# Another instruction order for a layernorm, multi-query attention and SiLU feed-forward kernel: the table that sets the order is replaced

## The chip, the core and the metric

The kernel runs on one core of one Trainium2 chip. The metric is the device time of one execution in microseconds (us), from three executions. TensorE is called PE in the profile, VectorE DVE, ScalarE ACT, GpSimd POOL and SyncE SP; PEld is the loading of weights into PE.

## What is computed

```python
def _A_ref(x, wq, wk, wv, wo):              # S 2048, D 640, H 32 heads of Dh 20, one key and value head
    q = (x @ wq).reshape(B, S, H, Dh).transpose(0, 2, 1, 3)
    k = x @ wk
    v = x @ wv
    scores = jnp.einsum("bhqd,bkd->bhqk", q, k) * (Dh ** -0.5)
    p = _softmax(scores, axis=-1)
    o = jnp.einsum("bhqk,bkd->bhqd", p, v)
    return o.transpose(0, 2, 1, 3).reshape(B, S, H * Dh) @ wo

def _B_ref(x, w1, w2):                      # F 1728
    return jnp.einsum("bsf,fd->bsd", _silu(jnp.einsum("bsd,df->bsf", x, w1)), w2)

xn = _layernorm(x, axis=-1)
return x + _A_ref(xn, A_wq, A_wk, A_wv, A_wo) + _B_ref(xn, B_w1, B_w2)
```

## The kernel before, in words

**The work and its pieces.** The 32 heads are taken in 8 groups of 4, and the 2048 queries in 4 chunks of 512, which makes 32 attention groups. Each attention group runs over 16 key tiles of 128. One *item* is one head, one key tile and 512 queries: a score matrix of 128 keys by 512 queries, which fills one of the 8 banks of PSUM (tile `psall`). There are 2048 items.

- **Scores (S), L1211.** An item's scores are one matmul that uses 32 of PE's 128 rows (a head has 20 channels). Matmuls for four different heads stand in four different row groups and run side by side. In the order they read `MATMUL psall<-sbt 128x512`.
- **Exponential, on ACT or on DVE.** Most items go to ACT: one ACTIVATE (L1301) takes one, two or three neighbouring banks (512, 1024 or 1536 columns). The others go to DVE and POOL: DVE makes an exponential by integer arithmetic from one bank (L1533, called p1), and for each four such items two shifted copies are made, either both on POOL (L1572) or one of them on DVE (L1577). The three copies weighted together correct the coarse exponential.
- **Weighted values (PV), L1336.** Four matmuls of 512 columns, one for each head of a group, side by side in four column groups of PE. One such set belongs to each key tile done by ACT, and three to each key tile done by DVE, one for each copy.
- **Projections and feed-forward, L536** (and L823): all in sets of four matmuls in the four column groups. q, h (first feed-forward layer), out (second layer and output projection together), and for the last query chunk y, w and fin. ACT makes a tanh (L862) and DVE a product (L865) for each bank of h.

PE thus runs in two ways: **row mode** for scores (four row groups) and **column mode** for nearly all else (four column groups). A set of four in either mode streams 512 columns. In the order printed below, a run of scores stands as one row, for instance `L1211 ... x4`: four scores, for ACT and DVE together.

**What sets the order.** The program is straight-line, 22826 instructions in the profile. `build` holds a planner: it keeps a clock for each engine, reckons with a duration for each instruction (`t_act`, `t_dve`, `t_mc`, the table `WAY` for the way from one engine to another, `SWITCH` for a change of PE's mode), and puts instructions in a fixed sequence for each engine; `emit` then writes these sequences with the semaphore waits between them. After 36000 ns on the planner's clock (`HAND`) the planner no longer chooses: PE's sequence is read from the string `ORDER`, and `OTHERS` says in which order DVE, ACT and POOL take the kinds of their instructions. A token of `ORDER` has three characters. `S24` is a run of scores for ACT into two banks from bank 4 on, `S3x` and `S1x` into three and one; `D32` or `E12` is one score for DVE (E: with one of the shifted copies on DVE); `a`, `d` are a set of PV for a key tile of ACT or DVE; `n` begins a job of projection or feed-forward, `m` is its next set. The number of S, D and E tokens also sets how many items go to ACT and how many to DVE.

Where the clocks enter while `ORDER` is followed: an instruction's earliest start, and so which engine's next token is placed first. What runs on the chip is only the resulting sequence of each engine; the chip knows none of the planner's times.

**The end.** The last attention group ends with its last PV. ACT then copies the sums (L1434), PE adds up over the heads (`sum31`, L1132), DVE takes reciprocals (L1135), PE spreads them (`spread31`, L1150), DVE multiplies (L1159), and PE ends the five output banks (`fin0` to `fin4`, in part before and in part behind the spread, L536). DVE (L1100) and for bank 0 ACT and POOL (L1096, L1097) make the result, and four DMAs store it (L1117).

The lines on which most hangs:

```python
def t_act(n):                                     # L250
    return 64.0 + 0.8333 * n
def t_mc(n):                                      # L258: a column set
    return n / 2.4 + (9.0 if n >= 512 else 4.0)
    def turn(self, mode):                         # L347: a change of PE's mode
        return SWITCH[mode] if mode != self.pe_mode else 0.0
        if e == "pe" and not replay["on"] and not replay["at"] and ORDER and sc.t["pe"] >= HAND and cur_job[0] is None and not pro:
            replay["on"] = True                   # L2217: from here ORDER is followed
```

Of the kernel before, what the change touches and what calls it, by code (L numbers as in the profile page):

```python
# [22 lines left out]
QW = 512  # L23
# [35 lines left out]
DVE_END = 85.0  # L59
# [22 lines left out]
SWITCH = {"s": 97.0, "p": 98.0, "f": 98.0}  # L82
SPRIO = 0.5
# [28 lines left out]
def rule(n):  # L112
# [4 lines left out]
    "D32D13S14a97nq6m00m00D25S20m00m00S22D34aa7S20Dd5nh6m00D04D22S13m00m00m00S20S14Dd5G33nh2m00m00m00m00S25D00D31nh4m00m00m00m00ab7S25D20S13nh2m00m00m00m00"  # L117
    "S25Dc1D14nh0m00m00m00m00ac7S21D23s25ad7ae7af7d04d14S31D30d34d24D85D16S17a04d44d64S10S21D33d54a14d94S25E20D97d74dc4S22D01d84df4S25D20D97a24da4nh1m00S22"
    "E30m00D05D26S17m00m00S22E30a34a44db4S25Dc7di4dd4S22D20dl4nh1m00S35de4S10D32Dc3m00m00dg4dj4m00S25E12S17nq0m00m00m00m00dh4S22D35D81a54a64S26D10a74S22D75"
    "nh1m00m00m00m00S25D20S17nh2m00m00dk4m00m00S25D11S13dm4nh7m00m00m00dn4m00S30D85G26nh3m00m00m00m00S24D27s20D12a06a16a26a36d06S24D33Da7d16d36S20D02d26d66"  # L120
    "S23D35a46d46S20E12D87a56d96d56S33D32d86S20D17a66dc6nh2m00S23Dc5D77m00m00m00da6S20E25d76nh3m00m00S24Dc7m00S20D12m00a76nq7m00S24D72m00m00db6m00S20D23a86"
    "S24D82a96df6S20D13E27de6dd6nh2S24D33m00D10E21S17m00m00m00S33S10nh7dh6m00m00m00dg6m00S11S24Db3a02a12d02d32d12S20D13D26d62d22S24D07a22a32S13S20Da6a42d52"
    "nh7m00m00S23D05D16m00m00a52d92d82S20D33De4a62S25d42d72da2S20D33De7dc2S25D04a72nh3m00S20D77m00S24E16m00m00S17D10De1a82db2S24E06a92dd2S20D17de2nh3m00S24"
    "D06m00m00aa2m00S26S10Da1F34nh5m00m00m00m00S22D06a07d07d37S20D34d27d17S22D15a17d67S20Da4D36d57d97S22D05a27d77S20Da4nh6m00m00S22D15m00a37S20D34d87D05E12"
    "S13m00nh4m00m00S20Dd5a47m00m00S22D06d47a57dc7S20D26Dd5da7df7S22E34db7S20D26a67dd7S24D02nh3m00m00S20Dd6m00a77S24E32de7dg7m00S20D26a87nq2m00m00S25D04m00"
    "m00S20D93a97dh7d04S25D32d14S20D23a04d34d24S25D02E37d64S20D93a14nh2m00S25D07m00D23S10D81m00m00a24S35D33nh0m00m00m00m00a34d54S31s25D17d94d74dc4d84d44D20"
    "S21E33a44da4Dc7S25D10a54db4S21D23nh7m00E35Dc0S16m00m00m00S21D13a64df4S25D30dd4nh3m00S21E27m00Dc0S15D26a74m00m00S21D17a84de4S25D30nh7m00S21D83m00m00S25"
    "D20a94dh4S31dg4m00a05d05d35d65D14s16S31nq0m00m00m00m00S26D34a15d25S21D90D23a25d15d45D04S26d55d95S20D92D63a35d75S26D34d85nq2m00S20Dd3m00S26D04m00m00S20"
    "D63a45a55S26E32D04dc5da5db5S20Dd2D63a65df5S26E34nq2m00S20Dd3m00m00S26D04m00a75S20D63a85dd5S26E32de5dg5S20D94a95dh5S22D06E37nq4m00S20D25m00m00S22D06m00"
    "a07d07S20D95d37d67S22D34D06d27S20D25a17a27S32G36d57a37d97S20S25d87dc7a47d17S22Da4F00D11d47d77a57S24Dc6G30S22da7D11S24Dc6a67df7D20s31db7S24D56a77E30s31"  # L130
    "Dc6de7D20S24G36a87S30a97dh7S34dd7dg7nq3m00m00m00m00S20D22a07d07S25D14D83a17d37S20D32d17d47S25D14D83a27d27S20D22d67E34s25D13a37d57S20D22d97a47S23D85G36"
    "S20D22d77da7a57S23D15dc7S20E36d87S22Dc4D15a67df7S20D26db7S22Dc4D55a77S20S16F34a87S22D25de7S20E34F86D15dh7S32a97dd7S20dg7d06d36S32D35G27a06a16S20D95d66"
    "S22D04D37d16no5m00m00m00S20E24m00m00S22D87m00m00m00D14S20m00m00m00d26m00S22S14D87m00m00m00m00m00a26a36S30D33m00a46a56d96d56S24D27d46S20D32Dc3d76da6d86"
    "S24D12E27a66dc6S20D33db6S24D12no7m00m00m00m00S20Dc3m00m00m00m00S24E22a76S20D33m00m00m00m00m00m00S32D25m00m00m00m00a86a96S20E15df6S22Da4D37dd6dg6S20D05"
    "no4m00de6S22Da7m00m00dh6S20D15m00m00m00m00S22D37Da6m00m00m00a05m00S20D07m00a15S22D76d05d15S20D17d35d25S22Da6m00m00a25S20D07m00m00m00m00S22D76a35d65S20"
    "E14D07d55d45S22De6a45a55S20E14D07a65d95S22D36d75d85S20E14Dc7dc5da5S22D26df5db5D14S20D87a75a85a95no2S23E36de5S20D17m00m00m00m00m00S23S26m00m00m00m00m00"
    "m00dh5S20D23D34m00m00m00m00dd5S26D83m00m00m00S20D24dg5a03S26D12a13a23a33S20E34Da5d03d33S26D02a43d13S20D34d63S35E12a53d23nq4m00S20Dc2m00m00m00S25D17d93"
# [60 lines left out]
    "port": (  # L198
        "ppppdpppppddpppddppppppdppdpppdpppddpppppdppppdppppddppppppddppppppdddpppppppdpppppdddppppddddppppdppppddppppdddpppdpdppppdppppppdddppppddpppppddpppdp"
        "ppppppdddpdppppppdddpppppdpdppppppppddpppdppppdpppppdpppppppdddppppddppppppppdddppdppppppddpppddpppppdddpppppddppppdppppdpppppdppppddppdddpppdpppppppp"  # L200
        "pdddppppppdddppppdppdpppppppppdddppppppddppdpdppppdppppdpdppppppppdppppdpppppdppddppppdpdp"),
}
ENDLEAD = 0.04
ENDFROM = 0.85
# [45 lines left out]
def t_act(n):  # L250
    return 64.0 + 0.8333 * n
# [2155 lines left out]
```

## Time and profile before

| what | value |
|---|---|
| time, median of 3 executions | 671.14 us (671.09 to 672.52) |
| the profiled execution's own time | 671.75 us |
| its span, first to last instruction | 669.9 us |
| granted PE clock | 1.0 |
| matmuls, score matmuls among them | 9919, 2048 |
| score items on ACT (527 of two banks, 62 of three, 88 of one) | 1328 |
| score items on DVE | 720 |

The span is the time between the first and the last instruction of the execution that the hardware profiler recorded; 1.85 us lie around it. A busy share is the union of an engine's recorded instructions. Instructions of one engine overlap in the record, since the next begins while the last one still writes: how long an engine is held by one is read from start to start, not from the mean duration. The ends of PE's matmuls are modelled.

### The profile page before, as it was taken

To read this page: it belongs to the slowest core of one execution; us is meant where nothing else is said; L and a number is where in the kernel's file an instruction comes from. 1 tells how busy PE (TensorE), PEld (TensorE's weight loads), DVE (VectorE), ACT (ScalarE), POOL (GpSimd) and SP (SyncE) were. 2 spreads that over 40 slices of the span, in tenths; PEclk is the share of its full clock that TensorE was granted. 3 is DMA by queue.
4 is the path that set the end of the run, shared out by engine and by line. 5 is a ranking of instruction groups with operands and counts; after the bars stand their busy time and mean duration, and the time that the engine had idled before them with its cause. 6 is when DMAs were issued, how large, how long until landed. Compare 5 with 4: busy or idle time off the path is not lost.

```text
span 669.9 us, 22826 instructions
## 1 busy us (share of the span) xinstructions
PE 660.0 (99%) x9919; PEld 240.1 (36%) x9919; DVE 632.8 (94%) x1103; ACT 652.7 (97%) x750; POOL 535.5 (80%) x322
## 2 busy tenths in 40 slices
PE   8999999999999999999999999999999999999997
PEld 5433332332223333333332333333333333344434
DVE  7899999999999999999999999999999999988885
ACT  6999999999999999999999999999999999999995
POOL 6647879888777888977889788878878888778863
PEclk9999999999999999999999999999999999999999
DMA  8652202222131223223222231122422202242021
GB/s 229 169 198 19 30 18 23 23 27 31 26 35 24 34 19 40 30 31 37 63 23 26 26 40 26 24 32 33 77 21 24 21 21 33 22 79 24 9 23 41
DMA packets 34242, 28.99 MB, mean 43 GB/s; under 512 B 15486, under 2 KB 29662, under 8 KB 34142
## 3 DMA queue, kind: packets, MB, share of 16 engines
q1 hardware_dynamic: 33854, 27.20, 26.6%
q8 instruction: 78, 1.28, 0.8%
q10 hardware_dynamic: 288, 0.33, 0.1%
q14 instruction: 22, 0.18, 0.1%
HBM read 11.09 MB, written 2.62 MB: 20 GB/s over the span
## 4 chain that ended last, share of the span: by engine, by line
PE 79%; ACT 10%; DVE 8%; POOL 1%; issue 0%; DMA 0%; DVEq 0%; POOLq 0%; ACTq 0%
PE psall L1336 28%; PE psall L1211 25%; PE psall L536 24%; ACT sbt L1301 9%; DVE sbt L1533 5%; DVE sbt L1577 1%; POOL sbt L1572 1%; PE psall L710 1%; PE psall L684 1%; DVE sbt L782 0%; DVE sbt L1385 0%; DMA sbt<-in_A_x_dram 0%; PE psall L1150 0%; PE psall L1132 0%; DVE sbt L1100 0%
## 5 line engine op out<-in xcount | busy, mean ns | idle before, releaser
L1301 ACT ACTIVATE sbt<-psall 128x1024 bf16<-128x1024 f32 (+2 forms) x677 | 622.7, 1042 | 3.7 <-PE psall L1211 2.7
L1572 POOL TENSOR_SCALAR sbt<-sbt 128x2048 int16<-128x2048 int16 x250 | 474.3, 1897 | 94.3 <-DVE sbt L1577 25.1
L1533 DVE TENSOR_SCALAR sbt<-psall 128x512 int16<-128x512 f32 x720 | 458.1, 681 | 21.0 <-PE psall L1211 16.4
L1336 PE MATMUL psall<-sbt 128*32 128x512 bf16 x3488 | 274.4, 384 | 0.8 <-POOL sbt L1572 0.2
L1211 PE MATMUL psall<-sbt 32*128 32x512 bf16 x2048 | 251.1, 384 | 2.8 <-ACT sbt L1301 1.1
L536 PE MATMUL psall<-sbt 128*32 128x512 bf16 (+4 forms) x3904 | 216.9, 331 | 0.1
L1211 PEld LDWEIGHTS psall<-sbt 32*128 32x128 bf16 x2048 | 69.1, 91 | 222.0 <-ACT sbt L1301 137.3
L536 PEld LDWEIGHTS psall<-sbt 128*32 128x32 bf16 x3904 | 84.5, 95 | 82.6 <-issue 40.2
L1336 PEld LDWEIGHTS psall<-sbt 128*32 128x32 bf16 x3488 | 71.0, 94 | 108.3 <-issue 73.9
L1577 DVE TENSOR_SCALAR sbt<-sbt 128x2048 int16<-128x2048 int16 x110 | 74.6, 710 | 0.2
L949 POOL TENSOR_TENSOR sbt<-sbt 128x512 bf16<-128x512 f32 x30 | 38.3, 1275 | 19.6 <-DVE sbt L1577 17.3
L865 DVE SCALAR_TENSOR_TENSOR sbt<-sbt,psall 128x512 bf16<-128x512 bf16 x52 | 35.2, 677 | 0.2
L862 ACT ACTIVATE sbt<-psall 128x512 bf16<-128x512 f32 x52 | 32.9, 633 | 0.0
L1385 DVE COPY sbt<-psall 128x512 f32<-128x512 f32 x31 | 21.2, 682 | 0.8 <-PE psall L1336 0.6
L782 DVE TENSOR_SCALAR sbt<-psall 128x512 bf16<-128x512 f32 x20 | 13.6, 680 | 0.5 <-PE psall L536 0.3
L661 POOL TENSOR_TENSOR sbt<-sbt 128x2 f32<-128x2 f32 x8 | 5.7, 708 | 8.6 <-DVE sbt L659 8.2
L992 DVE SCALAR_TENSOR_TENSOR sbt<-psall,sbt 128x320 bf16<-128x320 f32 x24 | 11.6, 485 | 0.6 <-PE psall L536 0.6
L674 POOL TENSOR_SCALAR sbt<-sbt 128x640 bf16<-128x640 bf16 x12 | 10.4, 874 | 1.5 <-DVE sbt L666 1.5
L652 DVE BATCH_NORM_STATS2 sbt<-sbt 128x6 f32<-128x320 bf16 x14 | 6.6, 473 | 2.0 <-DMA sbt<-in_A_x_dram 1.9
L684 PE MATMUL psall<-sbt 128*128 128x128 bf16 x80 | 6.9, 220 | 1.1 <-DVE sbt L677 1.1
L1835 PE MATMUL psall<-sbt 128*32 128x256 bf16 x144 | 6.8, 353 | 1.2 <-DVE sbt L576 1.2
L696 DVE COPY sbt<-psall 128x640 bf16<-128x640 bf16 x14 | 6.4, 482 | 1.0 <-PE psall L684 1.0
(59 smaller groups left out, 97.8 us busy)
## 6 DMA issues: line engine op xcount, KB each, us to landing
sbt<-sbt SPq DMA_DIRECT2D x120, 64.0 KB, 3.8
sbt<-in_A_x_dram SPq DMA_DIRECT2D x28, 160.0 KB, 3.9
sbt<-sbt SPq DMA_DIRECT2D x213, 20.0 KB
out_dram<-sbt SPq DMA_DIRECT2D x14, 160.0 KB, 1.9
sbt<-in_B_w_dram SPq DMA_DIRECT2D x1, 2160.0 KB, 12.2
sbt<-in_B_w_dram SPq DMA_DIRECT2D x1, 2080.0 KB, 8.1
sbt<-sbt SPq DMA_DIRECT2D x75, 8.0 KB
sbt<-in_A_wq_dram SPq DMA_DIRECT2D x1, 800.0 KB, 6.3
```

Source lines behind the costliest of these rows:

```text
L536: ins = pe.matmul(ps[j * SLOT:(j + 1) * SLOT, b * BANK + off:b * BANK + off + n], w[:, j * SLOT:(j + 1) * SLOT], x, start=start, stop=stop ...
L782: op = Op("dve", lambda v: v.tensor_scalar_mul(q_st[:, st, :], bk(job.bank), QSCALE), t_dve(512), DVE_END, pre=[job.ready], writes=[res("q ...
L862: t = Op("act", lambda a: a.activation(t_buf[0:rows, ts, :], bk(job.bank, 0, QW, rows=rows), AF.Tanh, scale=0.5), t_act(512), ACT_END, pre ...
L865: u = Op("dve", lambda v: v.scalar_tensor_tensor(out=hT[par][0:rows, fk, :], in0=t_buf[0:rows, ts, :], scalar=1.0, in1=bk(job.bank, 0, QW, ...
L949: nm = pool(lambda e: e.tensor_tensor(oU[:, us, :], U_sb[:, us, :], Rrep, ALU.mult), 1356.0, POOL_END, pre=[uc] + lc + pack_op.get(divmod( ...
L1211: return pe.matmul(bk(b), kT_rep[i * SLOT:(i + 1) * SLOT, kt * P:(kt + 1) * P], qT[i * SLOT:(i + 1) * SLOT, g % NQ, :], start=True, stop=T ...
L1301: return a.activation(Ebuf[:, es * QW:es * QW + w], ps[:, buf[0] * BANK:buf[0] * BANK + w], AF.Exp, scale=ESCALE)
L1336: ins = pe.matmul(ps[i * SLOT:(i + 1) * SLOT, ub * BANK:ub * BANK + QW], lhsT, rhs, start=(first and k < HG), stop=(last and k >= len(lst) ...
L1385: return v.tensor_copy(U_sb[:, us, :], bk(ub))
L1533: p1 = Op("dve", lambda v: v.tensor_scalar(z16[:, i * QW:(i + 1) * QW], bk(job.bank), ZBIAS, 0.0, ALU.add, ALU.max), t_dve(QW) + 2.0, DVE_ ...
L1572: op = pool(lambda v, t=t, j=j, zin=zin: v.tensor_scalar(t.bitcast(I16), zin, float(SHIFT[j]), 1.0, ALU.add, ALU.mult), POOL_SHIFT, POOL_E ...
L1577: op = dve(lambda v, t=t, j=j, zin=zin: v.tensor_scalar_add(t.bitcast(I16), zin, float(SHIFT[j])), t_dve(N, 4), prio=SPRIO - 0.01 * j, **args)
```

## The change

The strings `ORDER` and `OTHERS` are replaced, and with them some of the durations by which the planner reckons while it follows them. The diff, with the strings cut to the start of one (they differ from the first token on):

```diff
-WAY = {("act", "dve"): 32.0, ("dve", "pool"): 84.0, ("pe", "act"): 41.0, ("pe", "dve"): 72.0}
+WAY = {("act", "dve"): 32.0, ("dve", "pool"): 84.0, ("pe", "act"): 42.0, ("pe", "dve"): 72.0}
+HOT = {"on": False}
+FIRST = 10.0
 ORDER = (
-    "D32D13S14a97nq6m00m00D25S20m00m00S22D34aa7S20Dd5nh6m00D04D22S13m00m00m00S20S14Dd5G33nh2m00m00m00m00S25D00D31nh4m00m00m00m00ab7S25D20S13nh2m00m00m00m00"
+    "S12D33D14a97nq6m00m00S15S20D23m00m00nh2m00S23Dc5m00S16D30D11m00m00S23D35nh0m00m00m00m00D21S25Fc4S13nh2m00m00m00m00S25D10aa7ab7ac7S23D20E31ad7S25Dc2ae7"
...
 def t_act(n):
-    return 64.0 + 0.8333 * n
+    return (54.0 if HOT["on"] else 64.0) + 0.8333 * n
...
 def t_mc(n):
-    return n / 2.4 + (9.0 if n >= 512 else 4.0)
+    return n / 2.4 + (3.0 if HOT["on"] else 9.0 if n >= 512 else 4.0)
...
     def turn(self, mode):
-        return SWITCH[mode] if mode != self.pe_mode else 0.0
+        return (106.0 if HOT["on"] and mode == "s" else SWITCH[mode]) if mode != self.pe_mode else 0.0
...
                 start += self.turn(op.mode)
+                if HOT["on"] and op.mode != "s":
+                    op.occ += FIRST
...
-                t_dve(HALF) + 40.0, DVE_END, pre=[job.ready, xres_op[(qc, i)]] + [norm_op[n] for n in range(NT)], reads=[res("xres", i)], writes=[res("os", sl) if hf == 0 else res("os2", sl)],
+                t_dve(HALF), DVE_END, pre=[job.ready, xres_op[(qc, i)]] + [norm_op[n] for n in range(NT)], reads=[res("xres", i)], writes=[res("os", sl) if hf == 0 else res("os2", sl)],
...
-        op = Op("pe", f, 224.0, pre=[x[1] for x in d.values()] + v_op[kt // 4],
+        op = Op("pe", f, t_mc(QW) if HOT["on"] else 224.0, pre=[x[1] for x in d.values()] + v_op[kt // 4],
...
+    HOT["on"] = False
...
+            HOT["on"] = True
             replay["on"] = True
```

No instruction is of a new kind, and none changes its operands' sizes. Up to the first token of `ORDER` the sequences of all engines are the same. From there on they differ nearly everywhere. Counted over the whole program:

| instructions | before | now |
|---|---|---|
| ACT exponentials of two banks | 527 | 532 |
| ... of three banks | 62 | 65 |
| ... of one bank | 88 | 77 |
| DVE exponentials (p1) | 720 | 712 |
| shifted copies on DVE | 110 | 108 |
| shifted copies on POOL | 250 | 248 |
| PV matmuls | 3488 | 3472 |
| score matmuls | 2048 | 2048 |
| runs of scores between other matmuls (rows of L1211 in PE's order, L1215 now) | 591 | 573 |

All other groups have the same counts. Line numbers of the changed kernel are higher by 4 in this part of the source.

The first place is PE just behind the point from which the table rules, while projections of q (L536, now L540) stand between the scores (L1211, now L1215) and PV (L1336, now L1340). Before:

```order
L1336 MATMUL psall<-sbt 32x512 x4
L536 MATMUL psall<-sbt 32x512 x12
L1211 MATMUL psall<-sbt 128x512 x3
L536 MATMUL psall<-sbt 32x512 x8
L1211 MATMUL psall<-sbt 128x512 x3
L1336 MATMUL psall<-sbt 32x512 x4
L1211 MATMUL psall<-sbt 128x512 x3
L536 MATMUL psall<-sbt 32x512 x8
L1211 MATMUL psall<-sbt 128x512 x3
L536 MATMUL psall<-sbt 32x512 x12
```

And now:

```order
L1340 MATMUL psall<-sbt 32x512 x4
L540 MATMUL psall<-sbt 32x512 x12
L1215 MATMUL psall<-sbt 128x512 x4
L540 MATMUL psall<-sbt 32x512 x16
L1215 MATMUL psall<-sbt 128x512 x3
L540 MATMUL psall<-sbt 32x512 x4
L1215 MATMUL psall<-sbt 128x512 x3
L540 MATMUL psall<-sbt 32x512 x8
L1215 MATMUL psall<-sbt 128x512 x3
L540 MATMUL psall<-sbt 32x512 x20
```

The first run of scores shown takes four instead of three, sixteen column matmuls follow it instead of eight, and one PV set has left this place.

The second place is ACT, some 25 rows into its own order: the tanh of the first feed-forward layer (L862, now L866) between exponentials (L1301, now L1305) of one, two and three banks. Before:

```order
L1301 ACTIVATE sbt<-psall 128x1024
L862 ACTIVATE sbt<-psall 128x512
L1301 ACTIVATE sbt<-psall 128x1024
L1301 ACTIVATE sbt<-psall 128x512
L862 ACTIVATE sbt<-psall 128x512
L1301 ACTIVATE sbt<-psall 128x1024
L862 ACTIVATE sbt<-psall 128x512
L1301 ACTIVATE sbt<-psall 128x1024 x2
L1301 ACTIVATE sbt<-psall 128x1536
L1301 ACTIVATE sbt<-psall 128x512 x2
```

And now:

```order
L1305 ACTIVATE sbt<-psall 128x512
L866 ACTIVATE sbt<-psall 128x512
L1305 ACTIVATE sbt<-psall 128x1024 x5
L866 ACTIVATE sbt<-psall 128x512
L1305 ACTIVATE sbt<-psall 128x1024 x7
L866 ACTIVATE sbt<-psall 128x512
L1305 ACTIVATE sbt<-psall 128x1024 x4
L866 ACTIVATE sbt<-psall 128x512
L1305 ACTIVATE sbt<-psall 128x1024 x8
L1305 ACTIVATE sbt<-psall 128x512
```

The tanh instructions stand further apart, and fewer exponentials of one bank lie between them.

The third place is the end of PE's order, from the last run of scores on: `w4` and `fin0` (L536 with 32x512 between PV), the last PV, `fin1` (pieces of 128 and 384), `sum31` (L1132, now L1136) and `spread31` (L1150, now L1154). Before:

```order
L1211 MATMUL psall<-sbt 128x512 x3
L1336 MATMUL psall<-sbt 32x512 x4
L536 MATMUL psall<-sbt 32x512 x4
L1336 MATMUL psall<-sbt 32x512 x16
L536 MATMUL psall<-sbt 32x512 x8
L1336 MATMUL psall<-sbt 32x512 x4
L536 MATMUL psall<-sbt 32x128 x4
L536 MATMUL psall<-sbt 32x384 x4
L536 MATMUL psall<-sbt 32x128 x4
L536 MATMUL psall<-sbt 32x384 x4
L1132 MATMUL psall<-sbt 128x4 x4
L1150 MATMUL psall<-sbt 32x128 x16
```

And now:

```order
L1215 MATMUL psall<-sbt 128x512 x3
L1340 MATMUL psall<-sbt 32x512 x12
L540 MATMUL psall<-sbt 32x512 x4
L1340 MATMUL psall<-sbt 32x512 x4
L540 MATMUL psall<-sbt 32x512 x8
L1340 MATMUL psall<-sbt 32x512 x8
L540 MATMUL psall<-sbt 32x512 x8
L1136 MATMUL psall<-sbt 128x4 x4
L1154 MATMUL psall<-sbt 32x128 x16
L540 MATMUL psall<-sbt 32x128 x4
L540 MATMUL psall<-sbt 32x384 x4
L540 MATMUL psall<-sbt 32x128 x4
```

`fin0` has moved behind the last PV, and `fin1` from there to behind the spread; two more sets of `w4` stand before the last PV.

More of the change, by code (lines that the diff above doesn't have):

```diff
@@ new lines @@
+        "pppppspouppppppppppsspphhpphppsppphpphpphppuhppppppppppppphpphsphphpppppsshpuhqpppppppppppppppppsssopppppupqppppppppppppssspppsppoppppppsuppoppppppppp"
+        "pppsppppqppppppupppssopppppspppppppppssspoppppupsppopppppppppppppsqpppppsssppopupppppppppppqppppppppspppuppopppppppppppsshppppphpphsshpuppphpphpphppss"
+        "ppppppppppshpphpphphppupppshppppppppphpphhpssppppopppppppsspupoppppppspppppppppsspppopppupppsppopppppppposppppppppopuppsppoppppppopppsppppsupypppppppp"
+        "ypppppspppppyppppupppppypppwppwppwpswppssuppspyppppspppsgsw"),
@@ L202 @@
+        "ddppdpppdppppppdddpppppdddppppdppppddpppdppppppppppdpppddpppppppdddpppppppdddpdpppdpppppdpppppddppdpppdddpppdpppppdppdddppppppppdppppppddpppddpppppddp"
+        "ppdpppppdpppppddppppddpppdpppddppppdpppppdpppppdpppppdppdpppppppdppppppppppdppdddpdpdd"),
 }
```

152 lines of the change are left out of this document (73 added, 79 removed).

## The prediction

> **What bounds the kernel now.** The page's head and its shares come first.
>
> ```profile
> span 669.9 us, 22826 instructions
> PE 660.0 (99%) x9919; PEld 240.1 (36%) x9919; DVE 632.8 (94%) x1103; ACT 652.7 (97%) x750; POOL 535.5 (80%) x322
> PE 79%; ACT 10%; DVE 8%; POOL 1%; issue 0%; DMA 0%; DVEq 0%; POOLq 0%; ACTq 0%
> ```
>
> Three engines look full, so the busy shares settle nothing: they are unions of instructions that overlap in the record. The third row, the shares of the chain that ended last, says that 79% of the way back from the end runs over PE, 10% over ACT and 8% over DVE. To see how full an engine is, one must take its pace from start to start. For ACT these rows of the timeline stand side by side:
>
> ```profile
> 483.24 1.10 ACT L1301 ACTIVATE sbt<-psall 128x1024 bf16<-128x1024 f32 x1
> 484.14 0.69 ACT L862 ACTIVATE sbt<-psall 128x512 bf16<-128x512 f32 x1
> ...
> 502.40 1.45 ACT L1301 ACTIVATE sbt<-psall 128x1536 bf16<-128x1536 f32 x1
> 503.74 0.59 ACT L862 ACTIVATE sbt<-psall 128x512 bf16<-128x512 f32 x1
> 504.22 1.03 ACT L1301 ACTIVATE sbt<-psall 128x1024 bf16<-128x1024 f32 x1
> ```
>
> Two banks hold ACT for 484.14 - 483.24 = 0.90 us although the record shows 1.10; three banks for 503.74 - 502.40 = 1.34; one bank for 504.22 - 503.74 = 0.48. That is some 0.43 a bank and 0.05 an instruction. The groups of ACT in the stretch from 36 to 640 us, which the table rules and which has no tail in it:
>
> ```profile
> L1301 ACT ACTIVATE sbt<-psall 128x1024 bf16<-128x1024 f32 x498 | 473.7, 1061 | 1.4 <-PE psall L1211 0.9
> L1301 ACT ACTIVATE sbt<-psall 128x1536 bf16<-128x1536 f32 x54 | 79.7, 1479 | 0.3 <-PE psall L1211 0.2
> L1301 ACT ACTIVATE sbt<-psall 128x512 bf16<-128x512 f32 x84 | 51.5, 627 | 0.2
> L862 ACT ACTIVATE sbt<-psall 128x512 bf16<-128x512 f32 x52 | 32.9, 633 | 0.0
> ```
>
> 498 x 0.90 + 54 x 1.34 + (84 + 52) x 0.48 = 585.8 us of 604. ACT is thus 97% full, and some **18 us of waiting** hide in the overlaps, where the last column shows only 1.9. Here is what one such wait looks like (timeline, all engines):
>
> ```profile
> 565.24 3.95 ACT L1301 ACTIVATE sbt<-psall 128x1024 bf16<-128x1024 f32 x4
> ...
> 566.07 0.82 PE L1336 MATMUL psall<-sbt 128*32 128x512 bf16 x12
> ...
> 566.82 0.10 PEld L1211 LDWEIGHTS psall<-sbt 32*128 32x128 bf16 x4 [0.42 <-ACT sbt L1301]
> 566.82 0.40 PE L1211 MATMUL psall<-sbt 32*128 32x512 bf16 x4
> ```
>
> Four exponentials without a wait would take 3 x 0.90 + 1.10 = 3.80; they took 3.95. The first ended near 565.24 + 1.10 = 566.34 and freed its banks, yet the scores for these banks start at 566.82. In between PE was not idle: it streamed three PV sets from 566.07 on. The scores came late because the order had put them behind that work. The weight load's own wait (0.42 for ACT) had long ended by then. So PE's sequence, more than the length of ACT's work, holds ACT here.
>
> **The change, part by part.** Everything before the first token is the same, so only sums behind it count. PE's pace stands in these rows:
>
> ```profile
> 299.76 0.39 PE L536 MATMUL psall<-sbt 128*32 128x512 bf16 x4
> ...
> 300.09 0.39 PE L1211 MATMUL psall<-sbt 32*128 32x512 bf16 x3
> ...
> 300.42 0.61 PE L1336 MATMUL psall<-sbt 128*32 128x512 bf16 x8
> ...
> 300.96 0.44 PE L1211 MATMUL psall<-sbt 32*128 32x512 bf16 x4
> ```
>
> The second of two column sets ends 0.22 behind the first (0.61 against 0.39). A set before scores holds PE for 300.09 - 299.76 = 0.33, and scores before a set for 300.42 - 300.09 = 0.33. Each turn from one mode to the other thus costs 0.33 - 0.22 = 0.11, and a run of scores two turns, 0.22. PE has 18 runs fewer (591 to 573): 18 x 0.22 = 4.0. It has 16 PV matmuls fewer, four sets: 4 x 0.22 = 0.9. **PE: -4.9 us.** [...]
>
> ACT takes 8 items more, in 3 instructions fewer: 5 x 0.90 + 3 x 1.34 - 11 x 0.48 = +3.2. **ACT: +3.2 us.** DVE's pace:
>
> ```profile
> 174.09 3.67 DVE L1533 TENSOR_SCALAR sbt<-psall 128x512 int16<-128x512 f32 x6
> 177.68 1.28 DVE L1577 TENSOR_SCALAR sbt<-sbt 128x2048 int16<-128x2048 int16 x2
> 178.88 0.24 DVE L940 RECIPROCAL sbt<-sbt 128x16 f32<-128x16 f32 x1
> ```
>
> (177.68 - 174.09) / 6 = 0.60 for a p1 and (178.88 - 177.68) / 2 = 0.60 for a copy. 8 p1 and 2 copies fewer: **DVE -6.0 us.** POOL makes two copies fewer and is 80% busy; I take nothing for it, because what hides a later POOL is the spread between a copy and its PV, and that cover is not thinner with fewer copies.
>
> The **tail** is a term of its own:
>
> ```profile
> 661.08 0.40 PE L1336 MATMUL psall<-sbt 128*32 128x512 bf16 x4
> ...
> 661.31 0.61 PE L536 MATMUL psall<-sbt 96*32 96x128 bf16 x16
> 661.53 0.66 ACT L1434 ACTIVATE sbt<-psall 128x256 f32<-128x256 f32 x2 [0.50 <-PE psall L1336]
> 661.97 0.97 PEld L1132 LDWEIGHTS psall<-sbt 128*128 128x128 f32 x8 [0.33 <-ACT sbt L1434]
> ...
> 663.85 2.59 PE L536 MATMUL psall<-sbt 96*32 96x256 bf16 x72
> 664.74 2.48 DVE L1100 SCALAR_TENSOR_TENSOR sbt<-psall,sbt 128x512 bf16<-128x512 f32 x4 [0.21 <-PE psall L536]
> ```
>
> Between the last PV (661.08) and `sum31` (661.97) PE waits for ACT's copy, and `fin1` (the x16) fills the gap at no cost. In the new order `fin0`, two sets, fills it, and `fin1` stands in the last stretch, behind the spread, where PE runs without a break (the x72) and DVE follows it. `fin1` takes about 0.61 less the 0.2 by which a record outlasts its set: **+0.4 us**. That `fin0` leaves its old place gains nothing, since two `w4` sets take it, in the shadow of the last exponential.
>
> What these loads make of the time depends on who is last, and no row says that for an order that has not run. Two readings bound it. **By the chain's shares**, each engine's change counts with its share of the chain: 0.79 x -4.9 + 0.10 x +3.2 + 0.08 x -6.0 = -4.0. **By ACT alone**, as the fullest engine, it is +3.2. The share of the chain is nearer to what the rows show (PE streaming while ACT waits, a place of the kind at which PE has become lighter), but a lighter PE hands part of the chain to ACT, which has grown. So I give the chain's reading three parts in four: 0.75 x -4.0 + 0.25 x 3.2 = -2.2. With the tail -1.8, from the profiled execution's own 671.75 to 669.95; the median of the runs shown lies 0.61 lower, so the forecast is 671.14 - 1.8 = **669.3 us**. This asks that ACT's hidden waiting falls from 18 to some 18 - 3.2 - 2.2 = 12.6 us.
>
> Two things in the order speak for that much: runs of one bank leave ACT only 0.48 of work while the next scores are made, and there are 11 fewer of them; and the tanh instructions, whose scores need five column sets on PE first, stand further apart on ACT.
>
> **The rivals.**
>
> *ACT takes back all that PE gives (no change).* If the waits shrink by just as much as ACT's work grows, 3.2 and the tail's 0.4, the time stays: 671.1, give or take 1.3. For it: PE and ACT share 8 banks, and a lighter PE waits more often for ACT, as it does 375 times already:
>
> ```profile
> PEld psall L1211 <- ACT sbt L1301: 137.3, 375, 0.6
> PEld psall L1211 <- DVE sbt L1533: 37.7, 104, 0.9
> ```
>
> Most of these waits lie under running matmuls, like the one above.
>
> *ACT is the bound (slower).* The place is the stretch to 640 us, where 97% of ACT's time is work. If the order places scores no better than the old one did, the 18 us of waiting stay, and 3.2 + 0.4 = 3.6 are added: 671.14 + 3.6 = **674.7 us**. It decides when the waits shrink by less than 2.3 us, for then the time is up by over 1.3. Against it speaks that DVE, which holds the other part of the banks, and PE become lighter at once. [...]
>
> *The order fits much better.* If half of the 18 us goes: -9.0 + 3.6 = -5.4, 665.7 us. For it speaks only that waits like the one shown are a matter of sequence, not of work.
>
> *The table does not do what it says.* A sequence fixed beforehand meets durations that differ from those reckoned with. If a score is placed to be just in time and a copy or DMA lands later, PE stalls in order and both engines lose; then the time is that of the slower rival or above it.
>
> **How the numbers follow.** A gain of over 0.2% (1.3 us, about what a measurement of this kernel can tell from no change) comes from the forecast and from the better fit: 0.40 and 0.08. No change: 0.26. Slower: 0.26, the table's failure with it. The likeliest case alone spans 667.1 (the chain's reading without ACT's part, 671.14 - 4.0) to 669.8. The range must reach into both rivals: down to 666.2, a little short of the better fit, and up to 673.8, where the waits shrink by 0.9 only.
>
> **What would show it right or wrong.** The PE groups of the changed kernel must show the same 0.22 and 0.33; if a turn costs less there, PE's term is wrong. ACT's groups from 36 to 640 us, at 0.90, 1.34 and 0.48, should leave 12 to 13 us of waiting; 17 or 18 would make the slower rival right, under 10 the better fit. The chain's share of ACT should rise above 10%. In the tail, the last run of column sets should be longer by 16 matmuls and 0.4 us, and the time from the last PV to the end of the span as much longer. The prediction would be wrong at its root if DVE or a DMA, and not PE's sequence, ended most of the new waits.

## The result, and the profile after

The changed kernel took **675.45 us** (median of 4 executions, 674.33 to 675.55) against 671.38 (4 executions, 671.09 to 672.52) for the kernel before beside it: ratio **1.0054, 95% interval 1.0036 to 1.0071**. It became slower by some 4 us. The forecast was 669.3 with a range up to 673.8, so both the sign and the range were missed. The profiled execution took 674.33 us.

The head of the profile's page after the change, its clock row and the shares of the chain that ended last:

```profile
span 672.4 us, 22778 instructions
PE 661.4 (98%) x9900; PEld 241.0 (36%) x9903; DVE 630.2 (94%) x1093; ACT 654.4 (97%) x747; POOL 531.7 (79%) x320
PEclk9999999999989999999999999999999999999999
PE 62%; ACT 33%; DVE 3%; issue 0%; DMA 0%; POOL 0%; ACTq 0%
```

The busy shares say as little as before. The chain's do say something: ACT has risen from 10% to 33% and PE has fallen from 79% to 62%. In the clock row one slice of forty, the twelfth, stands at 8 where the kernel before had full speed throughout.

The groups of ACT between 36 and 640 us, where the prediction had set its test:

```profile
L1305 ACT ACTIVATE sbt<-psall 128x1024 bf16<-128x1024 f32 x497 | 476.2, 1084 | 2.3 <-PE psall L1215 1.7
L1305 ACT ACTIVATE sbt<-psall 128x1536 bf16<-128x1536 f32 x60 | 90.5, 1514 | 0.3
L1305 ACT ACTIVATE sbt<-psall 128x512 bf16<-128x512 f32 x71 | 44.0, 633 | 0.0
L866 ACT ACTIVATE sbt<-psall 128x512 bf16<-128x512 f32 x52 | 33.3, 642 | 0.0
```

By the paces of the prediction this is 497 x 0.90 + 60 x 1.34 + (71 + 52) x 0.48 = 586.7 us of work in 604, so **17.3 us of waiting** against 18.2 before. The forecast needed 12.6; 17 or 18 had been named as the sign of the slower rival.

The clock's dip lies in the stretches around 190 us. These are the windows of the changed kernel, with the busy time and count of PE, PEld, DVE, ACT and POOL, then the granted clock, the DMA share and GB/s:

```profile
188.00:191.50 3.50, 3.03 (x21) 0.77 (x20) 3.45 (x7) 3.50 (x5) 2.47 (x2) 1.00 0.41 47
191.50:195.00 3.50, 3.49 (x30) 0.93 (x30) 3.05 (x5) 2.87 (x4) 1.57 (x2) 0.52 0.02 5
```

And this is the first of these stretches in the kernel before, with a lean one just ahead of it:

```profile
184.00:188.00 4.00, 3.33 (x31) 1.00 (x27) 3.90 (x7) 4.00 (x4) 3.57 (x2) 1.00 0.89 64
188.00:191.50 3.50, 3.50 (x57) 1.20 (x54) 3.50 (x7) 3.50 (x4) 1.24 (x1) 1.00 0.16 36
```

From 188 to 191.5 us the new order leaves PE only 21 matmuls, where the old one had 57. For 3.41 us, from 191.47 us on, the granted clock is 0.50. PE and ACT in that stretch (timeline of the changed kernel):

```profile
193.00 1.92 PE L540 MATMUL psall<-sbt 128*32 128x512 bf16 x16
194.86 0.39 PE L1215 MATMUL psall<-sbt 32*128 32x512 bf16 x3
...
195.29 2.11 ACT L1305 ACTIVATE sbt<-psall 128x1024 bf16<-128x1024 f32 x2 [0.92 <-PE psall L1215]
```

Four column sets take 1.92 us, where the paces of full speed make it 3 x 0.22 + 0.39 = 1.05. The scores behind them come late, and ACT stands still for 0.92 us.

The execution on record had one such stretch, and the other three had more: their mean clocks were 0.994 and 0.995 against 0.997. The results list clock and time of each execution, and the two go together, in this kernel as in its repetition below: 673.46 us at 0.999; 674.33, 674.54 and 675.03 at 0.997; 675.39 to 675.55 at 0.994 to 0.995; 677.22 to 677.53 at 0.989. So the change cost two things: about 2.4 us at full clock (673.46 - 671.1, though that is one execution only), and about 2 us more in the median by halved stretches. At full clock the time would lie just inside the forecast's range, but on the wrong side of the kernel before.

### The profile page after: what moved, and what is told of

The parts are those of the page before. It is cut to its first block, busy times and chain, and to the rows that moved or that the text cites. A ratio compares the mean times of both kernels' runs of the same rounds, so it can differ in the third digit from the quotient of the medians.

```text
span 672.4 us, 22778 instructions
## 1 busy us (share of the span) xinstructions
PE 661.4 (98%) x9900; PEld 241.0 (36%) x9903; DVE 630.2 (94%) x1093; ACT 654.4 (97%) x747; POOL 531.7 (79%) x320
## 4 chain that ended last, share of the span: by engine, by line
PE 62%; ACT 33%; DVE 3%; issue 0%; DMA 0%; POOL 0%; ACTq 0%
ACT sbt L1305 31%; PE psall L1340 22%; PE psall L1215 20%; PE psall L540 19%; ACT sbt L866 2%; DVE sbt L656 1%; DVE sbt L700 0%; DVE sbt L1537 0%; DVE sbt L658 0%; DMA sbt<-in_A_x_dram 0%; PE psall L827 0%; POOL sbt L665 0%; PE psall L1136 0%; DVE sbt L1104 0%; PE psall L714 0%
## 5 line engine op out<-in xcount | busy, mean ns | idle before, releaser
L1305 ACT ACTIVATE sbt<-psall 128x1024 bf16<-128x1024 f32 (+2 forms) x674 | 625.1, 1071 | 4.1 <-PE psall L1215 3.3
L1340 PE MATMUL psall<-sbt 128*32 128x512 bf16 x3472 | 271.5, 384 | 0.2
L1215 PE MATMUL psall<-sbt 32*128 32x512 bf16 x2048 | 250.8, 384 | 5.4 <-ACT sbt L1305 2.4
L540 PE MATMUL psall<-sbt 128*32 128x320 bf16 (+5 forms) x3904 | 218.4, 332 | 0.1
L1215 PEld LDWEIGHTS psall<-sbt 32*128 32x128 bf16 x2048 | 69.2, 91 | 224.7 <-ACT sbt L1305 136.0
L540 PEld LDWEIGHTS psall<-sbt 128*32 128x32 bf16 (+1 forms) x3904 | 85.1, 96 | 83.5 <-issue 37.5
L1340 PEld LDWEIGHTS psall<-sbt 128*32 128x32 bf16 x3472 | 70.4, 95 | 107.1 <-issue 73.9
L1581 DVE TENSOR_SCALAR sbt<-sbt 128x2048 int16<-128x2048 int16 x108 | 72.8, 707 | 1.5 <-PE psall L1340 1.2
L866 ACT ACTIVATE sbt<-psall 128x512 bf16<-128x512 f32 x52 | 33.3, 642 | 0.0
L944 DVE RECIPROCAL sbt<-sbt 128x16 f32<-128x16 f32 x30 | 7.3, 243 | 0.0
```

Of the source, the lines that this page charges most:

```text
L540: ins = pe.matmul(ps[j * SLOT:(j + 1) * SLOT, b * BANK + off:b * BANK + off + n], w[:, j * SLOT:(j + 1) * SLOT], x, start=start, stop=stop ...
L866: t = Op("act", lambda a: a.activation(t_buf[0:rows, ts, :], bk(job.bank, 0, QW, rows=rows), AF.Tanh, scale=0.5), t_act(512), ACT_END, pre ...
L1215: return pe.matmul(bk(b), kT_rep[i * SLOT:(i + 1) * SLOT, kt * P:(kt + 1) * P], qT[i * SLOT:(i + 1) * SLOT, g % NQ, :], start=True, stop=T ...
L1305: return a.activation(Ebuf[:, es * QW:es * QW + w], ps[:, buf[0] * BANK:buf[0] * BANK + w], AF.Exp, scale=ESCALE)
L1340: ins = pe.matmul(ps[i * SLOT:(i + 1) * SLOT, ub * BANK:ub * BANK + QW], lhsT, rhs, start=(first and k < HG), stop=(last and k >= len(lst) ...
L1581: op = dve(lambda v, t=t, j=j, zin=zin: v.tensor_scalar_add(t.bitcast(I16), zin, float(SHIFT[j])), t_dve(N, 4), prio=SPRIO - 0.01 * j, **args)
```

## The experiments

Two theories start from here. **The clock**: the new order has stretches in which PE gets little work, the clock is halved behind them, and that is what was missing from the sum. **The loads**: the terms of the sum had the wrong weights, because PE's lighter load buys next to nothing and ACT's longer work costs most of its length. The rival to both is that the new sequence simply fits worse, whatever the loads are. The experiments take the clock first, then each engine's load, in the old order and in the new one, and then the tail. All ratios are against the kernel before, executed beside them on the same chip.

### Does it repeat? (again)

The changed kernel with no edit.

> The changed kernel, unchanged, for more executions. Theory A (clock): its PE is so little used near 188 us and near 206 us that the granted clock halves there for 3.4 us at a time; one such stretch in the profiled execution (mean clock 0.997, 674.3 us), two in the others (0.994 to 0.995, 675.4 to 675.6 us). So the executions fall into two groups about 1.2 us apart that go with the mean clock, and the trace shows halved stretches at one or both of these places and nowhere else before the end. Theory B (ACT): the loss is ACT's added work and the tail; clock and time do not go together.

Measured: 676.13 us (673.46 to 677.53, 6 executions), ratio 1.0065 [1.0044, 1.0085]. Its profiled execution had a mean clock of 0.989. The head of its page, and four windows of it:

```profile
span 675.6 us, 22778 instructions
PEclk9999999999977999999999999999999999999999
```

```profile
186.40:189.80 3.40, 2.96 (x24) 0.88 (x23) 3.35 (x7) 3.40 (x4) 3.24 (x3) 1.00 0.69 78
189.80:196.60 6.80, 6.80 (x57) 1.57 (x55) 5.14 (x9) 5.42 (x6) 3.75 (x3) 0.50 0.05 11
...
206.90:210.30 3.40, 2.62 (x23) 0.64 (x19) 3.40 (x7) 3.40 (x5) 3.24 (x3) 0.99 0.38 45
...
210.30:217.10 6.80, 6.68 (x49) 1.40 (x49) 4.89 (x9) 5.35 (x5) 4.39 (x4) 0.50 0.01 1
```

There are two thin places, 24 and 23 matmuls in 3.4 us, and behind each the clock is halved for 6.83 us, twice as long as in the first trace. ACT is then busy 5.4 of 6.8 us. The slowdown repeats, and its size varies with the number and length of such stretches.

### Filling the thin places, and filling others (fill_thin, fill_thick)

Seventeen sets of four matmuls that add zeros to an open PV bank are put on PE ahead of PV sets in the changed kernel: in `fill_thin` at the two thin places (184 to 193 and 203 to 209 us), in `fill_thick` at places where PE is full (120 to 165 us).

```diff
+for i in range(4):      # ahead of each of 17 chosen PV sets
+    pe.matmul(ps[i * SLOT:(i + 1) * SLOT, bank * BANK:(bank + 1) * BANK], zero_t[:, 0:SLOT], zero_t[:, 0:512],
+              start=False, stop=False, tile_position=(0, i * SLOT))
```

> The changed kernel with one more set of four matmuls on zeros (added to the open PV bank, so the result stays) ahead of 17 PV sets between 184 and 193 us and between 203 and 209 us; the order of everything else stays. PE gets 17 x 0.22 = 3.7 us more work at places where it waits. Theory A: the mean clock is 1.000, the wait of 1.3 us on ACT near 193 us is gone, and the time falls to 672.6 (672.0 to 673.4). Theory B: added PE work can only hold or lengthen it: 675.4 to 676.5.

> The control for the run before: the same 17 sets, at PV sets between 120 and 165 us, where PE is well used. Theory A: the halved clock stays (mean 0.994 to 0.997), and the time is 675.4 plus part of the 3.7 us, 675.5 to 678. Theory B, or if the extra sets help by something else than the clock: the same as the run before.

Measured: `fill_thin` 674.06 us (674.05 to 674.16, 5 executions, every one at clock 1.000), ratio 1.0038 [1.0026, 1.0050]; `fill_thick` 677.38 (676.42 to 679.83, 6 executions, none above 0.997). The page and windows of `fill_thin`:

```profile
span 672.3 us, 22914 instructions
PEclk9999999999999999999999999999999999999999
```

```profile
188.00:191.50 3.50, 3.06 (x33) 0.82 (x29) 3.37 (x6) 3.50 (x4) 2.47 (x2) 1.00 0.39 46
191.50:195.00 3.50, 3.50 (x54) 0.99 (x46) 3.50 (x7) 3.50 (x5) 1.25 (x1) 1.00 0.02 5
```

With 33 matmuls instead of 21 ahead of it, the second window runs at 1.00 and PE does 54 matmuls in it instead of 30. The same matmuls elsewhere do not remove the dips; two windows of `fill_thick` show one of them:

```profile
208.50:211.90 3.40, 2.43 (x23) 0.73 (x19) 3.32 (x7) 3.40 (x5) 2.88 (x2) 1.00 0.15 26
211.90:215.30 3.40, 3.40 (x29) 0.71 (x29) 2.91 (x5) 3.08 (x3) 1.61 (x2) 0.50 0.02 5
```

So the halved clock came with the thin PE work of these places (0.50 behind 21 matmuls, 1.00 behind 33), and most of the spread of the times came from it. In size this was partly a miss: work was added and the time fell by 1.4 from the median, but 674.06 lies above the expected 672.0 to 673.4. Even at full clock the new order is about 2.4 us slower. The clock is only the smaller half of the answer.

### The same fill in the kernel before (before_fill)

Eight such sets near 184 to 188 and 202 to 205 us of the kernel before, where it is leanest.

```diff
+FILLS = (994, 998, 1002, 1004, 1065, 1069, 1073, 1076)      # positions of the PV sets in PE's order
```

> The kernel before with 8 more sets on zeros at its own two least used places, between 184 and 188 us and between 202 and 205 us. Theory A: the few executions at a mean clock of 0.997, which took 672.5 and 673.1 us, vanish; all lie at 1.000 and within 0.4 us of 671.0 to 671.4, and the median is the same or up to 0.4 us lower than before's. If the dips come from elsewhere, some executions still show 0.997.

Measured: 671.79 us (671.64 to 672.22, 12 executions, all at 0.999 or more), ratio 1.0002 [0.9993, 1.0011]. The kernel before, beside all experiments, fell below 0.999 in 11 of 55 executions and took 672.4 to 673.5 there instead of some 671.1; here none did. But the fill was expected to leave the median the same or lower, and it costs 671.79 - 671.15 = 0.6 us of the 8 x 0.22 = 1.8 that it adds, which eats the gain. It is no faster kernel. If the 17 sets of `fill_thin` cost as much, the new order at full clock stands at 674.06 - 0.6 = 673.5, which agrees with the one undisturbed execution at 673.46.

### More work on one engine of the kernel before (before_pe, before_act)

`before_pe` puts 23 zero sets, spread evenly, into the kernel before: 23 x 0.22 = +5.0 us of PE. `before_act` puts 54 tiny ACTIVATEs of 8 columns into it, ahead of 54 tanh instructions.

```diff
+FILLS = (387, 513, 643, ..., 2998, 3166, 3313)       # before_pe: 23 sets
```
```diff
+a.activation(tiny[:, 8 * k:8 * k + 8], zero_t[:, 0:8], AF.Copy)    # before_act: ahead of 54 tanh
```

> The kernel before with one more set of four matmuls on zeros ahead of 23 PV sets, spread evenly over the stretch that the table rules: 23 x 0.22 = 5.0 us more work for PE, as much as the change takes from it, and nothing else moved. By the chain's shares (0.79) the time rises by 3.9 us, to 674.9 from the 670.9 of executions at full clock. Theory B (ACT is the bound: adding 5.7 us of ACT work cost some 3.9) says that PE's work counts for little: under 1.5 us, 671.0 to 672.4.

> The kernel before with one tiny ACTIVATE (8 columns, a copy of zeros) ahead of each of the 54 tanh instructions: ACT gets some 54 x 0.06 to 0.10 = 3.2 to 5.4 us more work, in the same order, as much as the change adds. By the chain's shares, on which three quarters of the forecast rested, the time rises by 0.10 of it, 0.3 to 0.5 us (671.7 to 671.9). If ACT is the bound, it rises by nearly all of it, 3 to 5 us (674 to 676).

What the tiny instruction costs is read from start to start on ACT (timeline of `before_act`):

```profile
483.58 0.24 ACT L2255 ACTIVATE sbt<-sbt 128x8 bf16<-128x8 bf16 x1
483.70 0.61 ACT L862 ACTIVATE sbt<-psall 128x512 bf16<-128x512 f32 x1
...
485.56 0.25 ACT L2255 ACTIVATE sbt<-sbt 128x8 bf16<-128x8 bf16 x1
485.66 0.64 ACT L862 ACTIVATE sbt<-psall 128x512 bf16<-128x512 f32 x1
```

It holds ACT for 0.10 to 0.12 us, so 54 make +5.7 us. Measured: `before_pe` 674.91 us, ratio 1.0044 [1.0030, 1.0059], which is 3.7 us or **0.75** of the work added. `before_act` 675.30, ratio 1.0057 [1.0044, 1.0070]; at full clock 674.9 against 671.0, 3.9 us or **0.69** of the work. The chain of the kernel before gave PE 0.79 and ACT 0.10. For work added to PE that was right; for work added to ACT it was wrong seven times over.

### Less work on one engine of the kernel before (before_less_pe, before_less_act)

`before_less_pe` leaves out the last 26 of the 320 columns of each half in the output sets of the feed-forward and the projection: 1824 matmuls, 456 sets, 456 x 26/512 of a set's 0.21 to 0.22 us, some -4.9 us of PE, as much as the change takes away. `before_less_act` leaves out the last 76 columns of 48 tanh: 48 x 76/512 of a bank's 0.43 us, some -3.0 us of ACT.

```diff
-f = (e1 - e0, hT[par][:, fk, i * P:(i + 1) * P], w2_sb[:, fk, e0:e1])
+f = (e1 - e0 - 26, hT[par][:, fk, i * P:(i + 1) * P], w2_sb[:, fk, e0:e1 - 26])    # and wo_sb the same
```
```diff
+a.activation(t_buf[0:rows, ts, 0:436], bk(job.bank, 0, 436, rows=rows), AF.Tanh, scale=0.5)    # instead of 0:512
```

> The kernel before with the 456 output sets of 320 columns cut to 294; the last 26 columns of each half are left out of the computation. PE has 456 x 26 / 2.4 ns = 4.9 us less work in the same order, as much as the change took from it. If PE's work counts alike in both directions (23 sets more cost 3.7 for 5.0), the time falls by 3.6 us, from 671.1 at full clock to 667.5. Theory C (the two engines work in turns and what PE saves, ACT does not use): it falls by under 1 us, to 670.1 or more; then the loads alone explain the change. In between, a part of the change's loss belongs to the new sequence itself.

> The kernel before with 48 tanh instructions over 436 instead of 512 columns; the last 76 columns are left out. ACT has 3.0 us less work in the same order. From the changed kernel, where as much gave 1.75 us: 671.1 falls to 669.3. If PE's sequence holds the kernel before (theory of the forecast), 0.3 us: 670.8.

Measured: `before_less_pe` 670.62 us, ratio 0.9991 [0.9982, 1.0000]. That is 0.6 to 0.8 us for 4.9 us of PE, or **0.15** of the work. `before_less_act` 670.89, ratio 0.9994 [0.9985, 1.0002]: 0.3 to 0.6 us for 3.0 us of ACT, hardly more than nothing. The shares of the chain with less PE work (`before_less_pe`):

```profile
PE 67%; ACT 20%; DVE 8%; POOL 3%; issue 1%; DMA 0%; DVEq 0%; POOLq 0%; ACTq 0%
```

With more PE work (`before_pe`):

```profile
PE 88%; DVE 7%; ACT 3%; POOL 1%; issue 0%; DMA 0%; DVEq 0%; ACTq 0%
```

With less ACT work (`before_less_act`):

```profile
PE 75%; ACT 13%; DVE 10%; POOL 1%; issue 0%; DMA 0%; DVEq 0%; ACTq 0%
```

With more ACT work (`before_act`):

```profile
PE 50%; ACT 38%; DVE 9%; POOL 1%; issue 1%; DMA 0%; DVEq 0%; POOLq 0%; ACTq 0%
```

The two ACT runs act on the same tanh instructions. The two PE runs do not share theirs: the zero sets are spread evenly, and the shortened output sets lie between 200 and 600 us only. Their traces can be compared there by the start times of ACT's instructions, whose sequence is the same in both and in the kernel before. Over 200 to 280, 360 to 480 and 520 to 600 us together, ACT falls behind by 1.9 us in `before_pe`, for 11 sets or 2.4 us of work (0.8 of it), and gains 1.0 us in `before_less_pe`, for 4.5 us of work (0.2). So the difference is not one of the stretch. This is one traced execution each; 280 to 320 us is left out, since the traced execution of the kernel before lost 0.7 us there that those of `before_fill` and `before_less_act` did not.

Taking 4.9 us from PE moves the chain from 79% to 67% PE and from 10% to 20% ACT: where PE no longer ends last, ACT ends just behind it. The two engines are both nearly full, and the chain runs over whichever is last by a little. In this order PE's share told what *more* of PE costs; what *less* brings is limited by the distance to the next engine.

### Which engine holds the new order? (less_act, after_pe)

The same two questions in the changed kernel, both on top of `fill_thin`, so that the clock matters less: 48 tanh (the expectation says 47) over 436 columns (the last 76 columns left out, -3.0 us of ACT), and 22 more zero sets, spread (+4.8 us of PE). `fill_thin` ran on another chip than these two and the two runs on the tail below. The kernel before took 671.0 us at full clock there and 671.1 to 671.2 on theirs, so that differences from `fill_thin` are uncertain by some 0.2 us.

```diff
+a.activation(t_buf[0:rows, ts, 0:436], bk(job.bank, 0, 436, rows=rows), AF.Tanh, scale=0.5)    # less_act
```
```diff
+FILLS = (383, 515, 640, 776, 898, ..., 2849, 3013, 3165, ...)      # after_pe: 22 sets beside the 17
```

> The changed kernel with the 17 extra sets in its two thin places (674.06), and 47 of the tanh instructions over 436 instead of 512 columns; the last 76 columns of each are left out of the computation. ACT has 47 x 76 x 0.83 ns = 3.0 us less work, about what the change added to it (3.2), in the same order. Theory B: the time falls by 0.7 x 3.0 = 2.1 us, to 672.0 (671.5 to 672.6). If PE's sequence were what holds, as the forecast had it, it falls by 0.3 us, to 673.8.

> The changed kernel with the 17 sets in its thin places (674.06) and 22 more spread evenly, 4.8 us of PE work more. If the change has left PE with slack, it costs less than in the kernel before (3.7 for 5.0): 675 to 676. If the new sequence binds PE as much, 3.5 us: 677.6.

Measured: `less_act` 672.38 us, ratio 1.0018 [1.0007, 1.0028]; its executions at 0.999 or more took 672.23 to 672.40, which is 1.75 us below `fill_thin`, or **0.58** of the work taken away (in the old order 0.1 to 0.2). `after_pe` 676.31, ratio 1.0075 [1.0061, 1.0089], a little above the 675 to 676 expected: +2.25 us, or **0.47** of the work added (in the old order 0.75). The shares of the chain in `fill_thin`:

```profile
PE 64%; ACT 31%; DVE 4%; issue 0%; DMA 0%; POOL 0%; ACTq 0%
```

And in `after_pe`:

```profile
PE 76%; ACT 20%; DVE 2%; DMA 0%; issue 0%; ACTq 0%
```

The new order is held by ACT more and by PE less than the old one. Here PE's share of 64% said too much about added PE work (0.47). Five of the twelve executions of `less_act` and one of five of `after_pe` still had a clock of 0.997 or less; so had two of six and two of five in the runs on the tail below, which carry the same fill. In the traces of `less_act` and `after_pe`, the halved stretch follows the second thin place (0.50 from 209.4 to 212.8 us in the one, from 211.2 to 214.6 in the other): the fill there holds the clock up less surely than it seemed in `fill_thin`.

### The tail (tail, tail_other_bank)

The changed kernel with the fill, and `fin0` back ahead of the last PV as in the old order, so that `fin1` can lie beside ACT's copy: once in PSUM bank 0, once in bank 6.

```diff
-db7ab7")
+db7nf0m00ab7")      # tail; tail_other_bank: db7nf6m00ab7
```

> The changed kernel with the 17 extra sets (674.06), and fin0 ahead of the last PV, so that fin1 fills the gap between the last PV and sum31 as in the kernel before. The prediction's term for the tail says -0.4 us (673.7). If PE's end is not what the last stores wait for, 0.

> The run tail once more, with fin0 in bank 6 instead of bank 0. In bank 0 it had to wait for DVE to empty w4 (0.58 us on PE, and the last PV behind it came 1.2 us late). Without this wait the prediction's term for the tail gives 674.06 - 0.4 = 673.7.

Measured: `tail` 675.01 us, 0.95 **more** than `fill_thin`; `tail_other_bank` 674.34, no gain either. PE and ACT at the end of `tail`:

```profile
663.88 0.62 PE L541 MATMUL psall<-sbt 96*32 96x512 bf16 x8 [0.58 <-DVE sbt L1076]
664.33 0.39 PE L1341 MATMUL psall<-sbt 128*32 128x512 bf16 x4
...
664.76 0.66 ACT L1440 ACTIVATE sbt<-psall 128x256 f32<-128x256 f32 x2 [1.66 <-PE psall L1341]
```

`fin0` in bank 0 must wait until DVE has read the result of `w4` from that bank, and the last PV stands in order behind it. ACT's copy starts at 664.76; in `fill_thin` the same row reads

```profile
663.53 0.66 ACT L1440 ACTIVATE sbt<-psall 128x256 f32<-128x256 f32 x2 [0.50 <-PE psall L1341]
```

and stands 1.23 us earlier. A wait that was added to PE's queue held what stood behind it, and that was the last exponential's PV. In bank 6 there is no such wait, and from ACT's copy to the end of the span it is 8.38 us instead of 8.72, the 0.34 that was hoped for; but the copy starts 0.37 later, since two sets more stand ahead of it. So the tail's term was real, and neither of the two orders tried takes it back.

## Why the prediction was wrong, point by point

**The step that failed** is the one that turned loads into time: "By the chain's shares, each engine's change counts with its share of the chain", and three parts in four of that reading. It counted PE's -4.9 us at 0.79 and ACT's +3.2 us at 0.10; with the reading by ACT alone mixed in, at 0.59 and 0.33. The runs showed 0.15 for work taken from PE in the old order, 0.69 for work added to ACT there, and 0.58 for work taken from ACT in the new one. With the measured weights the same terms give -4.9 x 0.15 = -0.7 for PE, 3.2 x 0.58 to 0.69 = +1.9 to +2.2 for ACT and +0.3 for the tail: +1.5 to +1.8 us, against about +2.4 at full clock. That sum is an estimate from weights that were measured one engine at a time, on other instructions than those that the change moved, so it is no proof that the loads alone did it. The remaining 0.6 to 0.9 us is open, and with it the rival that the new sequence fits worse.

**A second step failed beside it**: the granted clock was put at nothing, without a reason. Halved stretches cost about 2 us in the median (675.45 against 673.46).

**PE: -4.9 us.** The counts and the paces hold. PE at full clock in the changed trace:

```profile
195.94 0.39 PE L1215 MATMUL psall<-sbt 32*128 32x512 bf16 x3
196.26 0.62 PE L1340 MATMUL psall<-sbt 128*32 128x512 bf16 x8
196.81 0.39 PE L1215 MATMUL psall<-sbt 32*128 32x512 bf16 x3
```

Scores ahead of a set hold PE for 0.32, and two sets ahead of scores for 0.55 = 0.22 + 0.33, as before. Left out was that the scores also stream in fewer sets of up to four (614 instead of 618, by the lengths of the runs), which by the same pace is some 0.9 us more. What was wrong above all is the worth of the term.

**ACT: +3.2 us.** The counts and the paces were right, and so was the warning that a lighter PE hands the chain to ACT. The share went far above the 10% named, to 33%. What was missing is how far: it was given one part in four.

**DVE: -6.0 us.** DVE has the work less, and waits more instead. Its exponentials in the page of the kernel before:

```profile
L1533 DVE TENSOR_SCALAR sbt<-psall 128x512 int16<-128x512 f32 x720 | 458.1, 681 | 21.0 <-PE psall L1211 16.4
```

And of the changed kernel:

```profile
L1537 DVE TENSOR_SCALAR sbt<-psall 128x512 int16<-128x512 f32 x712 | 455.2, 683 | 24.7 <-PE psall L1215 20.5
```

Its idle time ahead of them grew by 3.7 us; the waits for scores in it grew by 4.1. No run isolated DVE's term, so its weight stays open; these rows fit a weight near nothing.

**The tail: +0.4 us.** The last run of column sets, after the change:

```profile
663.73 0.66 ACT L1438 ACTIVATE sbt<-psall 128x256 f32<-128x256 f32 x2 [0.50 <-PE psall L1340]
...
666.05 3.03 PE L540 MATMUL psall<-sbt 96*32 96x128 bf16 x88
```

It has 88 matmuls instead of 72 and takes 3.03 instead of 2.59, 0.44 more; from ACT's copy to the end of the span it is 672.45 - 663.73 = 8.72 against 8.40, +0.3. Right, mechanism and size.

**Two things that were to shrink ACT's waits** (fewer runs of one bank, tanh further apart) did not: 17.3 us against 18.2. They were arguments from sequence without a price. The sign of an error at the root did not show: of the 2.3 us that the two-bank exponentials visibly waited, scores on PE ended 1.7.

**The clock was in no term.** The granted clock of the one execution shown was 1.0 throughout, and the order was not read for stretches where PE gets little. The thin stretches of the new order could have been found in PE's order; with how few matmuls the clock fell is known only from these runs (last section).

**The rivals.** "ACT is the bound" gave 674.7 and named the right engine and sign, with 17.3 us of waiting as it foretold. The agreement of its number is partly luck: its price took all of ACT's length; at full clock the kernel is about 1.2 us below that, and what brought the median to 675.45 was the clock. That the table fails to do what it says is not supported by these rows, in which the pieces run at the paces of before; it was not tested by itself. The sign of the change fits ACT as the bound. `before_less_act` does not fit it, where 3.0 us less on ACT brought 0.3 to 0.6 us: with two engines nearly full, relief of one alone gained little. The prediction called ACT the fullest and never worked out the same for PE. An estimate from its own paces, 558 runs of scores from 36 to 640 us at 0.44 with both turns and the column sets at 0.22 or by their columns, gives at least 585 us of 604 for PE, as much as ACT's 585.8.

No kernel that computes everything beat both: `before_fill` equals the kernel before, and `before_less_pe` and `before_less_act` leave work out.

## What to carry to other kernels

Where two engines are both nearly full, the chain's share of an engine is no weight for changes of its load. For the engine that leads the chain it was near the cost of *added* work once (0.75 against a share of 0.79) and too high once (0.47 against 0.64), and far off for work taken *away* (0.15 against 0.79); for the engine that is second it said far too little about added work (0.69 against 0.10). In an exchange between such engines, the side that gets work should here have been reckoned at some two thirds of it, and the side that loses work at little. And an order is to be read for its thinnest few microseconds on PE, not only for its sums, with the granted clock of several executions beside it.

## What the runs showed of the hardware

The granted clock of PE fell from 1.00 to 0.50 with no long gap on it: the longest in the thin stretches of the changed kernel are 0.30 and 0.36 us. The second of them is

```profile
209.50 0.39 PE L1215 MATMUL psall<-sbt 32*128 32x512 bf16 x3 [0.36 <-ACT sbt L1305]
```

The traces record the granted clock with the start and the length of each stretch, and in them the changes lie on a grid. In the changed kernel's first trace the full clock ahead of the halved stretch lasts 184.32 us, 54 times 3.413, the halved stretch 3.413, and the full clock behind it 477.87, 140 times 3.413. In the repetition the two halved stretches last 6.827 us each and begin 20.48 us apart, twice and six times 3.413. The grid did not begin with the kernel: the first edge on record lies at 7.15 us in the first trace, at 5.46 in the repetition and at 5.34 in the kernel before. Each trace divided into windows of 3.413 us on its own grid, with the matmuls that begin in each:

| window, from (us) | matmuls begun | clock in it | clock in the next |
|---|---|---|---|
| first trace of the change, 188.06 | 20 | 1.00 | 0.50 |
| ... 191.47 | 30 | 0.50 | 1.00 |
| ... 205.13 | 28 | 1.00 | 1.00 |
| ... 208.54 | 24 | 1.00 | 1.00 |
| `again`, 186.37 | 21 | 1.00 | 0.50 |
| ... 189.78 | 23 | 0.50 | 0.50 |
| ... 193.20 | 31 | 0.50 | 1.00 |
| ... 206.85 | 19 | 1.00 | 0.50 |
| ... 210.26 | 21 | 0.50 | 0.50 |
| ... 213.68 | 28 | 0.50 | 1.00 |
| kernel before, 182.83 | 25 | 1.00 | 1.00 |
| ... 203.31 | 24 | 1.00 | 1.00 |

The 14 traces have 2477 such windows between 36 and 640 us. The clock was half behind the eight with 19 to 23 matmuls and full behind all others, which have 24 or more; the leanest of `fill_thin` has 29. So in these traces 23 or fewer in a window went with a clock of 0.50 in the next, with 1.00 as with 0.50 in the window itself, and the two stretches of 6.83 us are those whose first window was thin as well (23 and 21). The leanest windows of the kernel before have 24 and 25, and its clock was below 0.999 in 11 of 55 executions. Where the edges fell went with it too: the second thin stretch of the first trace was spread over two windows, with 28 and 24, and had no dip; in the repetition it lay in one, with 19, and had one. The recorded busy time of PE does not separate the two groups. The window with 20 is busier than the one with 24 (2.96 us against 2.63; a view's x also counts a matmul that only reaches into the window):

```profile
188.06:191.47 3.41, 2.96 (x21) 0.77 (x20) 3.36 (x7) 3.41 (x5) 2.41 (x2) 1.00 0.40 47
208.54:211.95 3.41, 2.63 (x24) 0.81 (x24) 3.33 (x7) 3.41 (x4) 1.90 (x1) 1.00 0.00 0
```

The division between 23 and 24 is read from traces, in which up to three matmul records are missing, and was not tested by itself. It was seen with matmuls of these shapes: ahead of 36 us, where others run, a window with 20 (`before_act`, from 31.54 us) was not followed by a clock of 0.50.

The halved stretches lasted 3.41 or 6.83 us, one or two of the same unit, at a clock of 0.50, and the mean clock differed from one execution to the next (0.989 to 0.999 in the repetition). Why few matmuls go with the lower clock, and what sets the unit, was not shown.

Executions with a clock of 0.996 or 0.997 took 1.1 to 1.4 us more than the others in `less_act` (673.4 to 673.7 against 672.3). In the kernel before it was 1.2 to 1.6 us in seven of the eleven, and 1.9 to 2.4 in four, against the median at full clock on the same chip. At a clock of 0.50 PE loses 1.7 us in a dip of 3.41 us, so most of that loss or all of it reaches the time, in a kernel in which 4.9 us less of PE's work brought 0.7.
